# One more pair of feed-forward blocks per chunk pair in the seven-product down projection, and another order of the first chunk pair's blocks

## The chip, the cores and the metric

The kernel runs on one core of a Trainium2 chip. The metric is the device time of one execution in microseconds (us); the time before is the median of three runs. A core has these engines, which run side by side and wait for each other by semaphores: TensorE (PE, matmuls), VectorE (DVE), ScalarE (ACT), GpSimd (POOL) and SyncE (SP, which here issues nearly all DMA transfers). PSUM is the memory in which matmuls leave their results; DVE and ACT read it, POOL does not in this kernel.

## The reference

One pre-norm transformer layer in float32 on 2048 tokens of width 640: attention of 32 heads, then a SwiGLU feed-forward part of width 1728.

```
x = A_x
h = x + _A_ref(_layernorm(x, axis=-1), A_wqkv, A_wo)
h2 = h + _B_ref(_layernorm(h, axis=-1), B_w_gate, B_w_up, B_w_down)
...
def _B_ref(x, w_gate, w_up, w_down):
    g = _silu(x @ w_gate)
    u = x @ w_up
    return (g * u) @ w_down
```

## The kernel before

Projections, attention and the output projection take the first three quarters of the span; the change concerns the feed-forward part behind them, and the splitting of the down weights, which POOL does in tasks spread over attention (`prepare_weights`).

**Numbers.** To keep float32 accuracy every matmul operand is split into a high and a low part (`split`: ACT writes the high part, POOL or DVE the low one), and a product is the sum of high x high, high x low and low x high: three matmuls.

**Tiling.** The 2048 tokens form four chunks of 512 (0 to 3), taken as two *chunk pairs*, pair 0 (chunks 0, 1) and pair 1 (chunks 2, 3). The width 1728 forms 14 blocks f: 0 to 12 are whole (128 columns), 13 is half (64). `ELEMENTS` lists (pair, f): for each pair first block 13, then 0 to 12, so 28 elements, numbered 0 to 27. An element computes the gate and up products of one block for both chunks of its pair (`blocks`; `plain` for block 13), 54 matmuls of 512 columns over eight steps (30 over six steps for block 13), and leaves y = silu(gate) x up for the first chunk ahead of its step 5 and for the second ahead of its step 7 (block 13: steps 2 and 5). Steps are called by element and number here: step 4.5 is element 4, step 5, counted from 0. The order of the whole stage is written out by hand: the tile framework runs under a manual schedule, so each engine executes its instructions in the order of the program.

**Down products.** A block's y is multiplied by its down weights for four *tile pairs* (tp 0 to 3, two tiles of 128 tokens each; tp 0 and 1 are the pair's first chunk). Work for one tile pair is a `Group`, and groups wait in the list `waiting`. A group of one block (`plain` in `Group`, for blocks for which `own` holds) has four products of three matmuls of 320 columns (two for block 13), and DVE adds each to h, the residual, in SBUF. A group of two blocks (`seven`) forms the 2x2 by 2x2 block product of two tiles, two blocks and two halves of the output with seven products in place of eight; three products are added to h, four to sums kept aside (`sums`, tiles named own). Before, pair 0 takes blocks 0, 1, 12 and 13 alone and 2 to 11 as pairs; pair 1 takes 10 to 13 alone and 0 to 9 as pairs.

A group of two needs its operands prepared (`prepare`): ACT splits and POOL adds and splits into tiles named yp, from a pool that is opened (`opened`) only when the list `late` is empty. `late` holds the work that turns chunks 2 and 3 into the layout of the products (normalise, transpose on PE, `sums` and `keep`, and stores to DRAM, among them those of the tile named kept), one entry per step; it empties in step 4.3. The memory of that work is then reused by yp. Blocks whose y is needed before that are split at once (`EARLY`).

After the last group of two, `put_together` appends eight POOL additions per tile pair to the list `chores`, which combine the sums aside with h. Then h is complete but for the blocks that are still to come; the last block's `plain` stores it to the output. Chunks 2 and 3 have no place of their own in the feed-forward part: their h lies in DRAM (h_d), and `bring_back` reloads it into the place of chunk 0 or 1 once that is stored.

**What sets the order.** After the up matmuls of each step, `step()` refills the weight rings on the SP queue (`unit_ring` of eight up-weight units, `down_ring` of ten down-weight pieces), calls `bring_back`, takes as many down products from `waiting` as `RATES` says for that element (14 by default, spread over its steps; a second number gives the first step), prepares, pops two chores, and pops one entry of `late`. What is left at the end is taken in the last loop over `waiting`. SP works in order too: a store that waits for POOL holds the loads behind it. Down products use four PSUM banks (ps_b), up products four others (ps_a); PE waits when DVE has not emptied one.

Of the kernel before, what the change touches and what calls it, by code (L numbers as in the profile page):

```python
# [11 lines left out]
F32R = mybir.dt.float32r  # L12
# [5 lines left out]
P = 128  # L18
# [9 lines left out]
TPC = CH // P  # L28
NF = (F + P - 1) // P
# [6 lines left out]
HALF = D // 2  # L36
# [8 lines left out]
def tile_block(ctx: ExitStack, tc: tile.TileContext, x, wqkv, wo, wg, wu, wd, out):  # L45
    nc = tc.nc
    x = x[0]
    out = out[0]
    ctx.enter_context(tc.manual_schedule())

    dram = ctx.enter_context(tc.tile_pool(name="dram", bufs=1, space=bass.MemoryType.DRAM))
# [9 lines left out]
    t_d = [dram.tile([P, 8 * CH], F32R, name=f"t_d{i}") for i in range(2)]  # L61
    w_d = [dram.tile([P, 8, 4 * P], F32R, name=f"w_d{f}") for f in range(NF)]
    d_d = {
        f: dram.tile([P, 2, 2 * HALF], F32R, name=f"d_d{f}") for f in (0, 1, *range(NF - 4, NF))
    }
    j_d = [dram.tile([P, 7, 2 * HALF], F32R, name=f"j_d{j}") for j in range((NF - 2) // 2)]
    h_d = dram.tile([2, P, TPC, D], F32, name="h_d")
# [903 lines left out]
    h_c = {c: pe1.tile([P, TPC, D], F32, name=f"h{c}") for c in range(2)}  # L971
# [302 lines left out]
        def free(self, n=1):  # L1274
            self.freed += n

    ELEMENTS = [(pair, f) for pair in range(2) for f in (NF - 1, *range(NF - 1))]

    def weight_rings():
        def unit(f, i):  # L1280
# [103 lines left out]
    for u in range(NU):  # L1384
        g, c = divmod(u, NC)
        if g == NG - 1 and c >= 2:
            _, first, ln, flips, _ = ahead
# [143 lines left out]

    def own(pair, f):

        return f >= NF - 4 if pair else f < 2 or f >= NF - 2

    SLOTS = ("A11", "A12", "A22", "S1", "S2", "S3", "S4")
    sums, chores, stored = {}, [], []
    waiting, pools = [], []

    class Group:  # L1540
# [48 lines left out]
        def seven(self, n):  # L1589
            name, _, place = SEVEN[n]  # L1590
            if self.tp == 0:
                self.d.append(down_ring.take())
            d, k = self.d[n], SLOTS.index(name)
            y_hi, y_lo = self.parts[:, 0, k], self.parts[:, 1, k]
            ps = self.multiply([(y_hi, d[:, 0]), (y_hi, d[:, 1]), (y_lo, d[:, 0])])
            if self.tp == 3:
                down_ring.free()
            if isinstance(place, tuple):
                self.add(ps, *place)
            else:  # L1600
                own_sum = sums[self.tp][place]
                if self.fs[0] == (2, 0)[self.pair]:
                    nc.vector.tensor_copy(own_sum, ps)
                else:
                    nc.vector.tensor_tensor(out=own_sum, in0=ps, in1=own_sum, op=ALU.add)
            if n == 6 and own(self.pair, self.fs[1] + 1):
                self.put_together()

        def put_together(self):

            h = h_c[self.c]
            at = [h[:, self.t + i, k * HALF : (k + 1) * HALF] for i in range(2) for k in range(2)]
            one, six, seven, five = sums[self.tp]
            for out, x in (
                (at[0], one), (six, one), (at[1], six), (at[1], five), (seven, six),
                (at[2], seven), (five, seven), (at[3], five),
            ):
                chores.append((
                    self.pair, self.tp,
                    lambda o=out, x=x: nc.gpsimd.tensor_tensor(out=o, in0=o, in1=x, op=ALU.add),  # L1620
                ))

        def plain(self, n):
            i, half = divmod(n, 2)
            if len(self.d) < 2:
                self.d.append(down_ring.take())
            d = self.d[half]
            cols = slice((self.t + i) * P, (self.t + i + 1) * P)
            if self.fs[0] == NF - 1:
                y = self.parts[:, cols]  # L1630
                pairs = [(y, d[:, 0]), (y, d[:, 1])]
            else:
                if isinstance(self.parts, tuple):
                    y_hi, y_lo = (y[:, cols] for y in self.parts)
                else:
                    y_hi, y_lo = self.parts[:, 0, i], self.parts[:, 1, i]
                pairs = [(y_hi, d[:, 0]), (y_hi, d[:, 1]), (y_lo, d[:, 0])]
            ps = self.multiply(pairs)
            if self.tp == 3 and i == 1:
                down_ring.free()  # L1640
            self.add(ps, i, half)
            if self.fs[0] == NF - 2 and half == 1:
                while any(c[:2] == (self.pair, self.tp) for c in chores):
                    chores.pop(0)[2]()
                tt = self.c * TPC + self.t + i
                nc.sync.dma_start(out[tt * P : (tt + 1) * P, :], h_c[self.c][:, self.t + i, :])
                if self.pair == 0:
                    stored.append((self.c, self.t + i))

    def prepare_some():  # L1650
        for n, g in enumerate(waiting[:3]):
# [3 lines left out]
    def next_down():  # L1655
        if not waiting:
            return
        g = waiting[0]
        prepare_some()
        f, i = g.steps.pop(0)  # L1660
        f(i)
        if not g.steps:
            waiting.pop(0)
# [127 lines left out]
    plan = []  # L1791
    for pair, f in ELEMENTS:
        if own(pair, f):
# [116 lines left out]
    def spread_over(n, steps, first=0):  # L1910
# [1 line left out]
        return [0] * first + [n * (i + 1) // m - n * i // m for i in range(m)]  # L1912

    RATES = {
# [3 lines left out]
    }  # L1918
    again = []

# [5 lines left out]
        again[:] = stored  # L1926
        stored.clear()

    EARLY = ((0, 0), (0, 1))

    def y_place():
        return pd2.tile([P, CH], F32, name="y", tag="y", bufs=7)
# [1 line left out]
    for e, (pair, f) in enumerate(ELEMENTS):  # L1934
# [5 lines left out]
        def step():  # L1940
# [12 lines left out]
            for _ in range(each[n]):  # L1953
                next_down()
            prepare_some()
            for _ in range(2):
                if chores:
                    chores.pop(0)[2]()
            if soon:
# [39 lines left out]
        before = ys  # L1999
    while waiting:  # L2000
        next_down()


_INS = ["A_x", "A_wqkv", "A_wo", "B_w_gate", "B_w_up", "B_w_down"]
# [26 lines left out]
```

## Time and profile before

| | |
|---|---|
| median of 3 runs | 2010.2 us (2009.26 to 2012.54) |
| the profiled execution's own time | 2009.57 us |
| its span in the trace | 2007.8 us |
| DVE, ACT and POOL busy | 80%, 71%, 40% of the span |
| feed-forward stage, elements 1 to 27 | from about 1492 us to the end |

The span is the time from the first to the last instruction in the trace. A row of the timeline reads: start in us, length in us, engine, line, operation, what is written and read, how many such instructions follow each other, and in brackets the engine's idle time before the row and what ended it. A row of a stretch reads: its bounds and length, then for PE, PEld (weight loads), DVE, ACT and POOL the busy us and the number of instructions, then the clock granted to PE, the busy share of the DMA engines and GB/s. A row of a group reads: busy us, mean ns of one, and idle time before.

### The profile page before, as it was taken

What the parts mean: (1) busy time and instruction counts of PE and PEld (TensorE: products, weight loads), DVE (VectorE), ACT (ScalarE), POOL (GpSimd) and SP (SyncE); (2) the same over time, 40 slices, a digit from 0 to 9 for tenths busy, and PEclk for the clock granted to TensorE, in tenths of its full rate; (3) what the DMA queues carried; (4) which work ended last, traced back from release to release, by engine and by line L of the source; (5) the groups of instructions that cost most, each with busy time, mean ns of one, the idle gap of its engine ahead of it and who ended that gap; (6) DMA issues with size and microseconds to landing.
All of it is one profiled execution on the core that took longest, in us unless ns stands there. A gap on an engine that the chain in (4) does not pass through costs nothing.

```text
span 2007.8 us, 40038 instructions
## 1 busy us (share of the span) xinstructions
PE 1998.6 (100%) x14346; PEld 1246.9 (62%) x14346; DVE 1603.0 (80%) x2806; ACT 1434.3 (71%) x2811; POOL 799.2 (40%) x1206
## 2 busy tenths in 40 slices
PE   9999999999999999999999999999999999999999
PEld 8999995333333333333334333345598888888888
DVE  5778778898898888989888989886387766676677
ACT  4678778999999999999999999986633222212221
POOL 7574423344343443453400020011156444854555
PEclk9999999999999999999999999999999999999999
DMA  8887563442634534435412031221158654974642
GB/s 250 259 265 258 180 218 82 128 147 92 188 107 140 154 128 145 157 121 178 154 50 77 27 94 53 79 63 62 50 189 300 227 181 161 358 266 158 205 150 94
DMA packets 201541, 310.98 MB, mean 155 GB/s; under 512 B 55960, under 2 KB 89816, under 8 KB 200320
## 3 DMA queue, kind: packets, MB, share of 16 engines
q1 hardware_dynamic: 194752, 284.83, 43.6%
q0 software_dynamic: 6496, 23.60, 3.9%
q8 instruction: 114, 1.87, 0.4%
q14 instruction: 83, 0.68, 0.1%
q10 hardware_dynamic: 96, 0.00, 0.0%
HBM read 208.73 MB, written 99.32 MB: 153 GB/s over the span
## 4 chain that ended last, share of the span: by engine, by line
PE 97%; DMA 1%; DVE 1%; POOL 1%; ACT 0%; issue 0%; SPq 0%; ACTq 0%; POOLq 0%; DVEq 0%
PE acc L1319 25%; PE ps_a L1487 17%; PE ps_one L1309 16%; PE ps_max L274 13%; PE ps_one L647 10%; PE ps_b L1582 9%; PE ps_max L239 3%; PE ps_max L1037 2%; PE ps_b L1037 1%; DMA q_d<-e 0%; PE ps_two L700 0%; PE ps_max L1072 0%; DMA o_t<-o_d 0%; PE ps_a L1853 0%; DVE st L139 0%
## 5 line engine op out<-in xcount | busy, mean ns | idle before, releaser
L1315 ACT ACTIVATE probs<-ps_one 128x512 f32<-128x512 f32 x2048 | 1056.0, 614 | 58.7 <-PE ps_one L1309 33.9
L280 DVE TENSOR_REDUCE mx<-ps_max 128x1 f32<-128x512 f32 x1472 | 924.8, 683 | 104.5 <-PE ps_one L1309 79.0
L1309 PE MATMUL ps_one<-q_stk,k_stk 62*128 62x512 f32 x2048 | 579.4, 448 | 0.3 <-ACT probs L1315 0.3
L1319 PE MATMUL acc<-probs,v_stk 128*32 128x512 f32 x4096 | 546.2, 604 | 0.0
L1309 PEld LDWEIGHTS ps_one<-q_stk,k_stk 62*128 62x128 f32 x2048 | 247.5, 184 | 441.8 <-ACT probs L1315 419.9
L274 PE MATMUL ps_max<-k_stk,q_stk 60*128 60x512 f32 x1472 | 373.9, 425 | 0.1
L274 PEld LDWEIGHTS ps_max<-k_stk,q_stk 60*128 60x128 f32 x1472 | 272.9, 186 | 25.4 <-DVE mx L280 0.6
L1704 DVE TENSOR_TENSOR tmp<-ps_a,tmp 128x512 f32<-128x512 f32 x208 | 141.2, 689 | 121.0 <-PE ps_a L1487 92.9
L261 DVE TENSOR_REDUCE mx<-ps_max 128x2 f32<-128x512 f32 x288 | 180.7, 684 | 60.8 <-PE ps_max L239 56.1
L1319 PEld LDWEIGHTS acc<-probs,v_stk 128*32 128x32 f32 x4096 | 80.9, 108 | 178.9 <-issue 166.7
L251 ACT ACTIVATE ps_max<-ps_max 128x512 f32<-128x512 f32 x288 | 151.9, 584 | 39.6 <-PE ps_max L239 38.4
L1582 PE MATMUL ps_b<-halves,yp 128*128 128x320 f32 x1032 | 178.7, 308 | 0.2 <-DVE h L1587 0.2
L1582 PEld LDWEIGHTS ps_b<-halves,yp 128*128 128x128 f32 x1032 | 165.1, 188 | 16.0 <-DVE h L1587 0.5
L1487 PE MATMUL ps_a<-t,units 128*128 128x512 f32 x624 | 162.5, 396 | 0.0
L1354 POOL TENSOR_TENSOR o<-o,rb 128x512 f32<-128x512 f32 x31 | 39.9, 1286 | 268.9 <-DMA q_stk<-m_d 145.3
L90 POOL TENSOR_TENSOR yp<-y,yp 128x256 fp32r<-128x256 f32 x96 | 60.3, 628 | 187.0 <-ACT yp L89 187.0
L1487 PE MATMUL ps_a<-z,units 128*128 128x512 f32 x516 | 133.9, 394 | 0.0
L1487 PEld LDWEIGHTS ps_a<-t,units 128*128 128x128 f32 x624 | 112.6, 188 | 18.5
L295 POOL CAST neg<-neg 128x16 fp32r<-128x16 f32 x30 | 5.9, 196 | 282.7 <-DVE neg L287 282.7
L1587 DVE TENSOR_TENSOR h<-ps_b,h 128x320 f32<-128x320 f32 x248 | 109.7, 480 | 5.8 <-PE ps_b L1582 4.4
L647 PE MATMUL ps_one<-z_hi,w_lo 64*128 64x512 f32 x380 | 111.9, 392 | 0.0
L647 PE MATMUL ps_one<-z_hi,w_hi 64*128 64x512 f32 x380 | 111.7, 393 | 0.0
(220 smaller groups left out, 2752.7 us busy)
## 6 DMA issues: line engine op xcount, KB each, us to landing
units<-w_d SPq DMA_DIRECT2D x186, 256.0 KB
w_d<-stage SPq DMA_DIRECT2D x106, 256.0 KB
halves<-j_d SPq DMA_DIRECT2D x70, 320.0 KB
j_d<-stage SPq DMA_DIRECT2D x42, 320.0 KB
raw<-k_d SPq DMA_DIRECT2D x64, 160.0 KB
k_stk<-k_d SPq DMA_DIRECT2D x64, 160.0 KB
q_stk<-q_d SPq DMA_DIRECT2D x64, 160.0 KB
raw<-q_d SPq DMA_DIRECT2D x54, 160.0 KB
```

The source lines that it names most:

```text
L251: nc.scalar.activation(ps, ps, AF.Relu)
L261: nc.vector.tensor_reduce(mx[:, b, :, t, kc], ps.rearrange("p (j n) -> p j n", j=2), axis=AX.X, op=ALU.max,)
L274: nc.tensor.matmul(ps, queries[u][rows, pair, t * P : (t + 1) * P], keys[u // NC][rows, pair, kc * CH : (kc + 1) * CH], start=True, stop=True,
L280: nc.vector.tensor_reduce(mxs[u][:, b, pair, t, kc : kc + 1], ps, axis=AX.X, op=ALU.max)
L647: nc.tensor.matmul(ps, a[rows], b[rows], start=(i == n == 0), stop=(i == 1 and n == last), skip_group_check=True,)
L1309: nc.tensor.matmul(ps, keys[u // NC][rows, p, kt * P : (kt + 1) * P], queries[u][rows, p, :], start=True, stop=True,)
L1315: nc.scalar.activation(probs[p][:, b, :], ps, AF.Exp, scale=scale)
L1319: nc.tensor.matmul(acc[32 * j : 32 * j + 32, :], values[u // NC][:, kt, j * VW : j * VW + 32], probs[j // 2][:, j % 2, :], start=(kt == 0) ...
L1487: nc.tensor.matmul(ps.rearrange("p (t n) -> p t n", t=TPC), w[k][:, i], z[k][:, :, j], start=(first and m == 0), stop=(last and m == len(n ...
L1582: nc.tensor.matmul(ps, a, b, start=(n == 0), stop=(n == len(pairs) - 1))
L1587: nc.vector.tensor_tensor(out=h, in0=ps, in1=h, op=ALU.add)
L1704: add = lambda out, ps, x: nc.vector.tensor_tensor(out=out, in0=ps, in1=x, op=ALU.add)
```

## The change

All pairs of whole blocks but the last whole block go through the seven products, in both chunk pairs: blocks 0 to 11 as six pairs, 12 and 13 alone. Pair 0 now begins with blocks 13 and 12, then 0 to 11; only block 12 is split at once (`EARLY`). Pair 0 therefore ends with a put-together, and the stores of its h become chores behind it (`finish`); in pair 1 block 12 stays last and stores as before. The rates of elements 1 to 5, 15, 16 and 25 to 27 are others, four chores are popped per step in elements 14, 15, 16 and 27 in place of two, and the last loop pops one chore per product. The separate down weights of blocks 0, 1, 10 and 11 (d_d) are no longer split and stored; the pairs' weights (j_d) were stored for all six pairs before, too.

```diff
     d_d = {
-        f: dram.tile([P, 2, 2 * HALF], F32R, name=f"d_d{f}") for f in (0, 1, *range(NF - 4, NF))
+        f: dram.tile([P, 2, 2 * HALF], F32R, name=f"d_d{f}") for f in range(NF - 2, NF)
     }
...
-    ELEMENTS = [(pair, f) for pair in range(2) for f in (NF - 1, *range(NF - 1))]
+    ELEMENTS = [(0, f) for f in (NF - 1, NF - 2, *range(NF - 2))]
+    ELEMENTS += [(1, f) for f in (NF - 1, *range(NF - 1))]
...
     def own(pair, f):
 
-        return f >= NF - 4 if pair else f < 2 or f >= NF - 2
+        return f >= NF - 2
...
-                if self.fs[0] == (2, 0)[self.pair]:
+                if self.fs[0] == 0:
                     nc.vector.tensor_copy(own_sum, ps)
...
+            for i in range(2) if self.pair == 0 else ():
+                chores.append((self.pair, self.tp, lambda i=i: self.finish(i)))
...
-            if self.fs[0] == NF - 2 and half == 1:
+            if (self.pair, self.fs[0]) == (1, NF - 2) and half == 1:
                 while any(c[:2] == (self.pair, self.tp) for c in chores):
                     chores.pop(0)[2]()
-                tt = self.c * TPC + self.t + i
-                nc.sync.dma_start(out[tt * P : (tt + 1) * P, :], h_c[self.c][:, self.t + i, :])
-                if self.pair == 0:
-                    stored.append((self.c, self.t + i))
+                self.finish(i)
+
+        def finish(self, i):
+            tt = self.c * TPC + self.t + i
+            nc.sync.dma_start(out[tt * P : (tt + 1) * P, :], h_c[self.c][:, self.t + i, :])
+            if self.pair == 0:
+                stored.append((self.c, self.t + i))
...
     RATES = {
-        1: (10, 2), 2: (12, 0), 3: (13, 0), 4: (13, 0), 5: (14, 2), 6: (13, 0),
-        14: (12, 0), 15: (16, 0), 16: (16, 0),
-        25: (18, 0), 26: (22, 0), 27: (26, 0),
+        1: (8, 2), 2: (10, 0), 3: (11, 0), 4: (13, 4), 5: (15, 0),
+        14: (12, 0), 15: (18, 0), 16: (15, 0),
+        25: (14, 0), 26: (18, 0), 27: (30, 0),
     }
...
-    EARLY = ((0, 0), (0, 1))
+    EARLY = ((0, NF - 2),)
...
-            for _ in range(2):
+            for _ in range(4 if e in (14, 15, 16, 27) else 2):
                 if chores:
                     chores.pop(0)[2]()
...
     while waiting:
         next_down()
+        if chores:
+            chores.pop(0)[2]()
```

Three places of the instructions' order follow; rows give line, operation, what is written and read, the size, and a count. In the changed kernel the lines lie one to eight further down (1582 becomes 1583, 1620 becomes 1621).

PE around its first product from a prepared operand (yp). Before, from step 4.6 to step 5.2:

```order
L1487 MATMUL ps_a<-z_1_5625,units 128x512 x6
L1487 MATMUL ps_a<-z_1_5625,lasts 128x512 x3
L1582 MATMUL ps_b<-halves,y 128x320 x6
L1487 MATMUL ps_a<-z_1_5625,lasts 128x512 x3
L1582 MATMUL ps_b<-halves,y 128x320 x6
L1487 MATMUL ps_a<-z_0_5624,units 128x512 x6
L1487 MATMUL ps_a<-t_21742,units 128x512 x6
L1487 MATMUL ps_a<-z_0_5624,units 128x512 x6
L1487 MATMUL ps_a<-z_0_5624,lasts 128x512 x3
L1582 MATMUL ps_b<-halves,yp 128x320 x6
```

Now, from step 4.0 to step 4.5:

```order
L1488 MATMUL ps_a<-z_0_5620,units 128x512 x6
L1488 MATMUL ps_a<-t_21706,units 128x512 x6
L1488 MATMUL ps_a<-z_0_5620,units 128x512 x6
L1488 MATMUL ps_a<-z_0_5620,lasts 128x512 x3
L1488 MATMUL ps_a<-t_21705,units 128x512 x6
L1488 MATMUL ps_a<-t_21706,units 128x512 x6
L1583 MATMUL ps_b<-halves,y 128x320 x9
L1488 MATMUL ps_a<-t_21705,units 128x512 x6
L1488 MATMUL ps_a<-z_0_5620,lasts 128x512 x3
L1583 MATMUL ps_b<-halves,yp 128x320 x9
```

The first product from yp stands in element 4 in place of element 5, two steps behind the last entry of `late`, and the first four steps of element 4 hold up products alone.

SP where pair 1's h takes the place of pair 0's (out is the output, h_d the h of pair 1 in DRAM). Before, from element 15 on:

```order
L1924 DMA h_5622<-h_d 128x640
L1646 DMA out<-h_5623 128x640
L1265 DMA lasts<-w_d_79 128x512
L1924 DMA h_5623<-h_d 128x640
L1646 DMA out<-h_5623 128x640
L1265 DMA units<-w_d_78 128x512
L1924 DMA h_5623<-h_d 128x640
L1646 DMA out<-h_5623 128x640
L1265 DMA units<-w_d_78 128x512
L1265 DMA halves<-j_d_96 128x640
L1924 DMA h_5623<-h_d 128x640
```

Now, the last two tile pairs of pair 0:

```order
L1652 DMA out<-h_5619 128x640 x2
L1265 DMA lasts<-w_d_79 128x512
L1265 DMA halves<-j_d_92 128x640 x2
L1265 DMA units<-w_d_78 128x512
L1265 DMA halves<-j_d_92 128x640 x3
L1930 DMA h_5619<-h_d 128x640 x2
L1265 DMA units<-w_d_78 128x512
L1265 DMA halves<-j_d_93 128x640
L1652 DMA out<-h_5619 128x640 x2
L1265 DMA units<-w_d_78 128x512 x2
L1930 DMA h_5619<-h_d 128x640 x2
```

A store used to follow DVE's addition of block 12, tile by tile; now two stores follow POOL's eight additions of a tile pair, and the reloads come behind them.

POOL at the end of the program (h<-h,own and own<-own are the additions of `put_together`, yp<-y of 128x256 the split for a plain group). Before:

```order
L90 TENSOR_TENSOR yp<-y,yp 128x256
L1620 TENSOR_TENSOR h_5623<-h_5623,own 128x320
L1620 TENSOR_TENSOR own<-own 128x320
L1620 TENSOR_TENSOR h_5623<-h_5623,own 128x320 x2
L90 TENSOR_TENSOR yp<-y,yp 128x256
L1620 TENSOR_TENSOR own<-own 128x320
L1620 TENSOR_TENSOR h_5623<-h_5623,own 128x320
L90 TENSOR_TENSOR yp<-y,yp 128x256
L1620 TENSOR_TENSOR own<-own 128x320
L1620 TENSOR_TENSOR h_5623<-h_5623,own 128x320
L90 TENSOR_TENSOR yp<-y,yp 128x256 x4
```

Now:

```order
L1621 TENSOR_TENSOR own<-own 128x320
L1621 TENSOR_TENSOR h_5619<-h_5619,own 128x320
L1621 TENSOR_TENSOR own<-own 128x320
L1621 TENSOR_TENSOR h_5619<-h_5619,own 128x320
L90 TENSOR_TENSOR yp<-y,yp 128x256 x2
L1621 TENSOR_TENSOR h_5619<-h_5619,own 128x320
L1621 TENSOR_TENSOR own<-own 128x320
L1621 TENSOR_TENSOR h_5619<-h_5619,own 128x320 x2
L1621 TENSOR_TENSOR own<-own 128x320
L1621 TENSOR_TENSOR h_5619<-h_5619,own 128x320
L1621 TENSOR_TENSOR own<-own 128x320
L1621 TENSOR_TENSOR h_5619<-h_5619,own 128x320
```

The additions used to lie among the splits of the plain blocks 10 to 12, with four splits behind them. Now each tile pair's eight follow one another; between the four eights lie one preparation (of tile pair 3) and two times two splits, ahead of them the preparation of tile pair 2, and the last eight additions are the last that POOL does.

## The prediction

> **What bounds the kernel now.** First the page's engine line, then the table of stretches for the feed-forward stage from element 1 on.
>
> ```profile
> span 2007.8 us, 40038 instructions
> PE 1998.6 (100%) x14346; PEld 1246.9 (62%) x14346; DVE 1603.0 (80%) x2806; ACT 1434.3 (71%) x2811; POOL 799.2 (40%) x1206
> ...
> 1492.00:1995.00 503.00, 503.00 (x2612) 438.77 (x2612) 356.83 (x685) 118.22 (x254) 274.76 (x394) 1.00 0.63 213
> ```
>
> PE is busy in all 503.00 us of that stretch. A modelled busy time alone would not prove density, so I read starts in PE's timeline:
>
> ```profile
> 1569.15 0.86 PE L1487 MATMUL ps_a<-z,lasts 128*128 128x512 f32 x3
> 1569.84 1.04 PE L1582 MATMUL ps_b<-halves,yp 128*128 128x320 f32 x6
> 1570.72 1.56 PE L1487 MATMUL ps_a<-t,units 128*128 128x512 f32 x6
> 1572.12 1.03 PE L1582 MATMUL ps_b<-halves,yp 128*128 128x320 f32 x6
> ```
>
> Six matmuls of 320 columns advance PE by 1570.72 - 1569.84 = 0.88 us, 0.1465 each; six of 512 by 1.40, 0.233 each. Steps of the stage last the sum of these, so PE is the bound and nothing is waited for: a matmul removed is a matmul won, and every wait that is added is paid in full.
>
> **The change, part by part.** *Matmuls.* Two plain blocks cost a tile pair 2x4x3 = 24 matmuls, a seven-product pair 21. One pair of blocks more for each of 2 chunk pairs and 4 tile pairs: 8x3 = 24 matmuls fewer, 24 x 0.1465 = **-3.5 us**.
>
> *Weights.* Eight stores of d_d and their splits on POOL go, all during attention. Two equal stretches there, with and without such work:
>
> ```profile
> 900.00:934.00 34.00, 34.00 (x244) 13.49 (x240) 30.41 (x51) 33.30 (x67) 18.72 (x28) 1.00 0.56 187
> 1034.00:1068.00 34.00, 34.00 (x240) 13.14 (x232) 30.21 (x51) 33.08 (x66) 1.29 (x2) 1.00 0.29 86
> ```
>
> PE and ACT are full in both whether POOL has 18.72 or 1.29 us of work; the removal is worth 0. Between elements 5 and 13, and 17 and 25, POOL gets eight preparations more in all (40 us against the 228 that it is free in the stretch above) and the queue six weight loads; both stay behind PE, which is no nearer to them there than before: 0.
>
> *The first seven-product group (element 4).* It needs prepared operands (yp), whose memory is opened only after the late tokens' last store, in step 4.3. Before, PE asked for them in step 5.2; now in step 4.5. In between PE issued 33 matmuls of 512 and 48 of 320 columns: 33 x 0.233 + 48 x 0.1465 = 14.7 us, so PE asks at 1569.84 - 14.7 = 1555.1. When can they be there?
>
> ```profile
> 1541.09 0.71 PE L1853 MATMUL ps_a<-ident,z 128*128 128x128 f32 x5
> ```
> ```profile
> 1554.44 0.52 SPq L1812 DMA_DIRECT2D t_d<-halves  x1
> 1555.78 0.72 SPq L1812 DMA_DIRECT2D t_d<-kept  x1
> ...
> SPq L1265 <- DMA t_d<-kept: 0.4, 1, 0.4
> ```
> ```profile
> 1562.00 0.62 ACT L89 ACTIVATE yp<-y 128x256 fp32r<-128x256 f32 x2 [7.03 <-DMA units<-w_d]
> 1565.05 0.63 ACT L89 ACTIVATE yp<-tmp 128x512 fp32r<-128x512 f32 x1 [2.44 <-POOL tmp L1575]
> ```
> ```profile
> 1564.98 0.46 POOL L90 TENSOR_TENSOR yp<-y,yp 128x128 fp32r<-128x128 f32 x1
> 1565.76 1.30 POOL L90 TENSOR_TENSOR yp<-tmp,yp 128x512 fp32r<-128x512 f32 x1 [0.32 <-ACT yp L89]
> 1567.01 1.19 POOL L90 TENSOR_TENSOR yp<-y,yp 128x256 fp32r<-128x256 f32 x1
> ...
> 1570.73 1.29 POOL L90 TENSOR_TENSOR yp<-tmp,yp 128x512 fp32r<-128x512 f32 x1 [0.33 <-ACT yp L89]
> ```
>
> The kept store was issued at 1555.78. SP waited 0.4 us for it ahead of its next issue, and ACT began yp at 1562.00 after 7 us idle: yp lies where "kept" lay, so the store's 6.0 us gate it (the profile names another DMA; the one SP waited for fits better). From ACT's start to the last piece on POOL are 1567.06 - 1562.00 = 5.06 us. The chain to the store starts at the transposes of step 3.5 (1541.09); 15 down matmuls fewer stand ahead of these now, so it moves 2.2 us earlier and the pieces are complete at 1564.9. The second product's third matmul wants them at 1555.1 + 5 x 0.1465 = 1555.8. PE loses **9.0 us**. Bounds: 11 if the chain doesn't move; 6 if the store takes the 3.9 us of the "out" store below and ACT gets to the copy 0.7 us sooner. I take 9.0, since the 6.0 us is this very store. Ahead of PE's wait nothing helps: DVE and ACT have only work that PE feeds, and the next group's preparation is queued behind the first on POOL.
>
> [...]
>
> *The change of chunk pairs (elements 14 to 17).* Plain block 12 of pair 0 used to stand between the last put-together and pair 1, giving POOL time. Now pair 1's block 13 follows at once, and the rows of h that it adds to are first stored and reloaded.
>
> ```profile
> 1732.55 1.55 PE L1487 MATMUL ps_a<-z,units 128*128 128x512 f32 x6
> ```
> ```profile
> 1739.45 0.63 ACT L89 ACTIVATE y<-tmp 64x512 fp32r<-64x512 f32 x1 [0.83 <-DVE tmp L1676]
> ```
> ```profile
> L1620 POOL TENSOR_TENSOR h<-h,own 128x320 f32<-128x320 f32 x40 | 37.1, 930 | 2.6 <-DVE h L1587 0.2
> L1620 POOL TENSOR_TENSOR own<-own 128x320 f32<-128x320 f32 x24 | 21.5, 896 | 0.1
> ...
> 1756.41 0.88 POOL L1620 TENSOR_TENSOR own<-own 128x320 f32<-128x320 f32 x1
> 1757.37 1.71 POOL L1620 TENSOR_TENSOR h<-h,own 128x320 f32<-128x320 f32 x2
> 1759.04 0.87 POOL L1620 TENSOR_TENSOR own<-own 128x320 f32<-128x320 f32 x1
> 1759.87 0.73 POOL L90 TENSOR_TENSOR yp<-y,yp 128x256 fp32r<-128x256 f32 x1
> 1760.56 2.27 POOL L1620 TENSOR_TENSOR h<-h,own 128x320 f32<-128x320 f32 x2
> ```
> ```profile
> 1762.79 0.34 SPq L1646 DMA_DIRECT2D out<-h  x1
> ...
> 1766.73 0.32 SPq L1924 DMA_DIRECT2D h<-h_d  x1
> ```
>
> Prices: one put-together addition 0.9 us (64 take 58.6 busy; four run from 1756.41 to 1759.87), a preparation 5.0 (1567.01 to 1572.02), a plain split 0.7. In this stretch all is told without the delay of element 4, which shifts it as a whole. Step 14.0 starts at 1732.55, less 12 matmuls (1.8): 1730.8. ACT's half of block 13's first split ended at 1739.45 + 0.63, 7.5 us after that step began, and the same 15 and 12 matmuls stand before it now: POOL takes over at 1738.3. From there its program holds two such splits (1.4 each, as for 128x512 above), two preparations and 32 additions: 2.8 + 10.0 + 28.8 = 41.6, ending at 1779.9. Two out stores (0.4 between them) with 3.9 us to landing (1762.79 to 1766.73, where the reload waits for it), then a reload of the same size: h is back at about 1788.5. PE has 138 matmuls of 512 and 117 of 320 columns to step 16.7's products, 49.3 us, and ends the first that needs this h at 1780.4. DVE stops at its addition, with all later evictions queued behind; PE has four ps_b banks and goes on for three more products and 12 matmuls (0.9 + 2.8) to 1784.1, then waits for 1788.5: **4.5 us**. Bounds 0.5 (a reload in no time) to 8 (out and reload at the 6.0 us above). I take the 3.9 twice. Behind the store that waits on SP stand loads of up weights; they run a whole element ahead (54 x 0.233 + 42 x 0.1465 = 18.7 us), more than the 8 or so that SP is held.
>
> *The end.* Before, the put-together of pair 1 followed blocks 8 and 9, three plain blocks ahead of the end. Now it follows 10 and 11.
>
> ```profile
> 1964.67 1.56 PE L1487 MATMUL ps_a<-t,units 128*128 128x512 f32 x6
> ```
> ```profile
> 1967.75 0.95 DVE L1708 TENSOR_TENSOR y<-tmp 128x512 f32<-128x512 f32 x1
> 1997.29 7.07 DVE L1587 TENSOR_TENSOR h<-ps_b,h 128x320 f32<-128x320 f32 x17
> ```
>
> Step 26.5 starts at 1964.67, less 27 matmuls that are not yet issued there (4.0): 1960.7. The y of its first chunk follows 1968.7 - 1964.67 = 4.0 later, at 1964.7. Only then can POOL begin: four preparations 20.1, 32 additions 28.8, four plain splits 2.8, together 51.7, in a program without gaps, to 2016.4. By the matmuls alone DVE's last addition would end at 2004.36 - 3.5 = 2000.8; now it waits for POOL's. One addition (0.6) and the last store (2007.8 - 2004.36 = 3.4) end the span at 2020.4 where it was 2007.8: **+12.6**, the 3.5 us of saved matmuls included. Bounds: 8 if additions take their 0.84 best and the first preparations are hidden, 15 if more of them take the 1.2 or so that 1760.56 shows.
>
> *Sum.* 9.0 + 4.5 + 12.6 = 26.1 on the profiled execution's 2009.57 us (span 2007.8 and 1.8 around it): 2035.7. The median of the runs is 0.6 above that execution: **2036 us**.
>
> **The rivals.** (1) *Not slower*: POOL and the stores keep up, and only the matmuls count: 2010.2 - 3.5 = 2006.7. For it speaks that POOL is idle 60% of the span; against it that the average is not the end: its 51.7 us would have to fit into 2000.8 - 1964.7 = 36.1, so it decides at instructions of 0.70 of their rows. 4%. (2) *Only the end costs*: the kept store lands before step 4.5, h is reloaded in time: 2010.2 + 12.6 = 2023. It needs the store 9 us earlier; its chain hangs on PE's transposes. 14%. (3) *PE restarts slowly after each wait.* The warming matmuls at the kernel's start (L809) show it:
>
> ```profile
> 3.00:5.00 2.00, 2.00 (x12) 2.00 (x11) 1.00 1.09 383
> 7.00:10.00 3.00, 2.97 (x27) 2.77 (x25) 1.00 1.07 361
> ```
>
> 12 matmuls of 128 columns in 2 us, later 27 in 3: about 1.9 times slower at first, though the granted clock reads 1.00 in both. If a wait of 9 us brings that back for some 3 us, it costs 1.5, and the wait of 4.5 us perhaps as much: 2039. No wait of PE of that length stands in this trace. 25%. [...]
> (4) That the change doesn't do what it says is excluded by the order of instructions: 24 matmuls are gone.
>
> **How the numbers follow.** Forecast 2036 with 52%, rivals 1 to 3 with 4, 14 and 25%, 5% for waits that I have not seen (a longer time). The range 2020 to 2044 takes in the forecast with its bounds (2010.2 + 6 + 0.5 + 8 = 2025 below, + 11 + 8 + 15 = 2044 above) and rivals 2 and 3. A measurement of this kernel tells 0.2% from no change, 4 us: slower 0.94, same 0.04, faster 0.02 (rival 1, at -0.17%, lies just inside the border).
>
> **What would show it.** Element 4 right: an idle time of PE of 6 to 11 us ahead of its first product from yp, released by ACT, then POOL. The change of pairs right: DVE's h addition waiting for h<-h_d, and PE idle a few us in elements 16 or 17. The end right: POOL without gaps in the last 50 us, its additions to h the last but DVE's, PE done over 8 us before the end. Wrong: a PE that is full to the end, or the chain of waits naming weights.

## The result and the profile after

| | before | after |
|---|---|---|
| median | 2010.2 us (2009.3 to 2012.5) | 2044.5 us (2044.1 to 2047.5) |
| span of the profiled execution | 2007.8 us | 2045.7 us |
| mean granted TensorE clock in it | 1.000 | 0.994 |

The changed kernel is slower, by a ratio of 1.0171 (95% interval 1.0159 to 1.0183), 34.4 us. The forecast was 26 us more; the direction and each of the three waits came, but 8.5 us were missing from the sum, and the time lies half a microsecond outside the range.

The engine line of the changed kernel's page, and the row of the same stretch that stood first in the prediction (PE's busy us are the first figure behind the length; the clock is the third from the right):

```profile
span 2045.7 us, 40026 instructions
PE 2007.8 (98%) x14322; PEld 1249.2 (61%) x14322; DVE 1600.5 (78%) x2798; ACT 1438.6 (70%) x2821; POOL 810.7 (40%) x1232
...
1492.00:1995.00 503.00, 488.56 (x2491) 422.73 (x2490) 340.26 (x649) 117.75 (x252) 254.92 (x383) 0.99 0.64 216
```

PE was busy in all 503.00 us of that stretch; now it lacks 14.4 of them. What it waited for from 1492 on, in us in total, times, and the longest one (before, this list was one row of 0.2 us):

```profile
PE ps_b L1583 <- POOL yp L90: 10.7, 7, 3.1
PE ps_b L1583 <- ACT yp L89: 4.7, 1, 4.7
PE ps_b L1583 <- DVE h L1588: 3.3, 1, 3.3
PE ps_b L1583 <- DMA halves<-j_d: 2.9, 2, 2.0
PE ps_b L1583 <- ACT tmp L1723: 0.5, 1, 0.5
PE ps_a L1488 <- ACT tmp L1723: 0.5, 1, 0.5
```

Three rows answer to the forecast: ACT and POOL at yp (element 4 and the end), DVE at h (the change of pairs). The fourth, down weights, was not in it, and the prediction had named it among its signs of being wrong. The two short waits for ACT lie in steps 17.1 and 2.1. Waits are less than what is lost, though, since PE is also slow behind them. I therefore take, for each step, its length in PE's timeline less its matmuls at the dense pace (0.2326 us for 512 columns, 0.1462 for 320). Element 4:

```profile
1558.55 1.56 PE L1488 MATMUL ps_a<-t,units 128*128 128x512 f32 x6
1559.95 0.86 PE L1488 MATMUL ps_a<-z,lasts 128*128 128x512 f32 x3
1565.47 0.87 PE L1583 MATMUL ps_b<-halves,yp 128*128 128x320 f32 x2 [4.66 <-ACT yp L89]
1568.21 1.17 PE L1583 MATMUL ps_b<-halves,yp 128*128 128x320 f32 x3 [1.87 <-POOL yp L90]
1569.82 1.43 PE L1583 MATMUL ps_b<-halves,yp 128*128 128x320 f32 x4 [0.44 <-POOL yp L90]
1571.05 1.95 PE L1488 MATMUL ps_a<-z,units 128*128 128x512 f32 x6
```

Step 4.5 lasts 1571.05 - 1558.55 = 12.50 us for 9 matmuls of each kind, 3.41: 9.1 lost, and 0.4 more in step 4.6, whose first six matmuls took 1.95 in place of 1.56. The same reckoning over the whole stage finds all places above 0.35 us:

| place | forecast | lost in the trace |
|---|---|---|
| 24 matmuls fewer | -3.5 | -3.5 |
| step 2.1 | | 0.6 |
| element 4 | 9.0 | 9.5 (steps 4.5, 4.6) |
| element 14 (added loads of weights: 0) | 0 | 5.7 (1.5, 2.7, 1.4 in steps 14.3 to 14.5) |
| change of pairs | 4.5 | 5.9 (4.1, 1.0, 0.7 in steps 16.7, 17.0, 17.1) |
| end, without the matmuls | 16.1 | 14.9 |
| sum | 26.1 | 33.1 |

The end is 1.3 + 2.3 + 7.4 us in steps 26.7, 27.5 and the tail (0.7 of before taken off), and 4.0 because the span ends 8.0 us behind PE's last matmul where it was 4.0. From element 1 to the end the trace takes 2045.7 - 1496.3 = 549.4 us against 2007.8 - 1491.6 = 516.2 before: 33.2 more, so the table is complete. The other 4.7 us of the two spans' difference arose before the feed-forward part. By the first activation of attention (L1316), 319.63 against 316.28, 3.35 us are lost, in projections where this one execution waited for loads:

```profile
PE ps_max L239 <- DMA raw<-q_d: 2.0, 2, 1.4
```

About 1.6 more come right behind that, where its granted clock was 0.58 from 322 to 326, and 0.3 are won back by element 1. That is no part of the change: element 1 starts at 1490.6 to 1492.4 in eleven of the twelve kernels below (1493.9 in the other), and the three other executions of the changed kernel have spans of 2042.3 to 2042.9.

*The clock.* The same stretches show the granted clock (third figure from the right) around two of PE's waits:

```profile
1555.00:1560.00 5.00, 5.00 (x27) 4.26 (x26) 2.81 (x5) 1.67 (x3) 1.89 (x2) 1.00 0.70 249
1560.00:1565.00 5.00, 0.81 (x4) 0.32 (x2) 2.66 (x6) 0.24 (x1) 0.00 (x0) 1.00 0.96 298
1565.00:1571.00 6.00, 3.22 (x9) 2.45 (x10) 0.98 (x2) 1.51 (x5) 5.27 (x10) 0.51 1.03 379
1572.00:1577.00 5.00, 5.00 (x30) 4.56 (x29) 3.04 (x6) 1.77 (x4) 3.41 (x6) 1.00 0.29 88
...
1804.00:1807.00 3.00, 2.98 (x9) 2.61 (x10) 2.90 (x6) 1.14 (x3) 0.93 (x2) 0.50 0.94 364
```

So rival 3 came too, beside the forecast and not in its place: behind these waits PE starts again at half clock (0.51 and 0.50 in the rows from 1565 and 1804). In windows of 1 us each such dip amounts to 3.4 us at half (the sum of what is missing is 1.71 a dip), two of them in a row in element 4.

### The profile page after: what moved, and what is told of

It is laid out like the page before. It is cut to its first block, busy times and chain, and to the rows that moved or that the text cites. A ratio compares the mean times of both kernels' runs of the same rounds, so it can differ in the third digit from the quotient of the medians.

```text
span 2045.7 us, 40026 instructions
## 1 busy us (share of the span) xinstructions
PE 2007.8 (98%) x14322; PEld 1249.2 (61%) x14322; DVE 1600.5 (78%) x2798; ACT 1438.6 (70%) x2821; POOL 810.7 (40%) x1232
## 4 chain that ended last, share of the span: by engine, by line
PE 91%; DMA 3%; POOL 3%; DVE 1%; SPq 1%; ACT 1%; issue 1%; POOLq 0%; DVEq 0%; ACTq 0%
PE acc L1320 25%; PE ps_one L1310 15%; PE ps_a L1488 15%; PE ps_max L274 13%; PE ps_one L647 9%; PE ps_b L1583 7%; PE ps_max L239 3%; PE ps_max L1037 2%; PE ps_b L1037 2%; DMA raw<-k_d 1%; POOL h L1621 1%; POOL yp L90 1%; SPq L176 1%; POOL own L1621 0%; DMA halves<-j_d 0%
## 5 line engine op out<-in xcount | busy, mean ns | idle before, releaser
L1316 ACT ACTIVATE probs<-ps_one 128x512 f32<-128x512 f32 x2048 | 1055.9, 613 | 60.7 <-PE ps_one L1310 35.7
L274 PEld LDWEIGHTS ps_max<-k_stk,q_stk 60*128 60x128 f32 x1472 | 272.9, 186 | 26.5 <-DVE mx L280 0.7
L1583 PE MATMUL ps_b<-halves,yp 128*128 128x320 f32 x1056 | 188.9, 313 | 19.0 <-POOL yp L90 10.7
L1583 PEld LDWEIGHTS ps_b<-halves,yp 128*128 128x128 f32 x1056 | 171.8, 191 | 38.9 <-POOL yp L90 12.8
L89 ACT ACTIVATE yp<-tmp 128x512 fp32r<-128x512 f32 x48 | 30.3, 632 | 129.7 <-POOL tmp L1576 129.7
L1588 DVE TENSOR_TENSOR h<-ps_b,h 128x320 f32<-128x320 f32 x208 | 95.6, 482 | 25.9 <-PE ps_b L1583 14.3
```

Of the source, the lines that this page charges most:

```text
L274: nc.tensor.matmul(ps, queries[u][rows, pair, t * P : (t + 1) * P], keys[u // NC][rows, pair, kc * CH : (kc + 1) * CH], start=True, stop=True,
L1316: nc.scalar.activation(probs[p][:, b, :], ps, AF.Exp, scale=scale)
L1583: nc.tensor.matmul(ps, a, b, start=(n == 0), stop=(n == len(pairs) - 1))
L1588: nc.vector.tensor_tensor(out=h, in0=ps, in1=h, op=ALU.add)
```

## Experiments

Each kernel is the changed one with the edit shown (excerpts), unless it says otherwise. Times are medians of four or five runs, beside runs of the kernel before on the same chip, whose medians lie between 2009.6 and 2011.0. Gains are told against the 2044.5 above, so differences of a microsecond or so between two kernels are not told apart.

**Which half of the change.** Pair 1 as before the change, then pair 0 as before it.

```diff
-        return f >= NF - 2
+        return f >= (NF - 4 if pair else NF - 2)
...
-        25: (14, 0), 26: (18, 0), 27: (30, 0),
+        25: (18, 0), 26: (22, 0), 27: (26, 0),
```

> Pair 1 as in the kernel before (blocks 10 and 11 alone, rates and additions of the end as before); pair 0 as changed. Theory A (the forecast's end is right at +12.6, and what the forecast missed lies in elements 4 to 17): the kernel before, 2010.2, less 12 matmuls (1.75), plus element 4 (9.5), elements 14 to 17 (5.7 and 5.8 in the changed trace) and about 1 ahead of the feed-forward part: about 2030.5. Theory B (the 8.5 us that the forecast missed are lost at the end): 2010.2 - 1.75 + 9.0 + 4.5 = 2022.

2031.7 us (2030.1 to 2032.2), ratio 1.0103 [1.0086, 1.0120]: theory A. The trace has the losses of element 4, element 14 and the change of pairs (9.9, 6.1 and 7.2 us by steps), and at the end no more than before (0.7).

```diff
-    ELEMENTS = [(0, f) for f in (NF - 1, NF - 2, *range(NF - 2))]
-    ELEMENTS += [(1, f) for f in (NF - 1, *range(NF - 1))]
+    ELEMENTS = [(pair, f) for pair in range(2) for f in (NF - 1, *range(NF - 1))]
...
-        return f >= NF - 2
+        return f >= NF - 2 if pair else f < 2 or f >= NF - 2
```

> Pair 0 as in the kernel before (blocks 0, 1, 12 and 13 alone, its order, rates and early splits); pair 1 as changed. Theory A: only the end costs, with 12 matmuls saved in place of 24: 2010.2 + 12.6 + 1.75 - 1 (POOL's stretch was 54.7 us in place of 55.7 to the end) = about 2023.5, and the granted clock is 1.00 but for the last 25 us. Theory B (the loss that the forecast missed lies at the end): 2032.

2023.6 us (2022.6 to 2025.6), ratio 1.0065 [1.0050, 1.0080]: theory A again. Only the end is lost (15.7 us by steps, all in element 27, of which 0.7 were lost before, too), and there the plain splits queue behind POOL's additions:

```profile
2009.57 3.57 PE L1582 MATMUL ps_b<-halves,yp 128*128 128x320 f32 x12 [5.11 <-POOL yp L90]
```

The two halves cost 21.7 and 13.6 us over 2010, together 35.3 where the whole change costs 34.4: they add to within a microsecond. For pair 1 the forecast has 12.6 + 1.75 = 14.4, so what it missed belongs to pair 0.

**Element 14.** The new wait, first on SP, then on PE, in the changed kernel:

```profile
1745.99 1.19 SPq L1265 DMA_DIRECT2D halves<-j_d  x2
1747.22 0.48 SPq L1911 DMA_DIRECT2D t<-t_d  x1
1747.80 1.89 SPq L1265 DMA_DIRECT2D halves<-j_d  x2
```
```profile
1754.30 1.50 PE L1583 MATMUL ps_b<-halves,yp 128*128 128x320 f32 x6 [0.90 <-DMA halves<-j_d]
1755.64 0.86 PE L1488 MATMUL ps_a<-z,lasts 128*128 128x512 f32 x3
1758.48 1.68 PE L1583 MATMUL ps_b<-halves,yp 128*128 128x320 f32 x6 [1.98 <-DMA halves<-j_d]
1759.95 2.77 PE L1488 MATMUL ps_a<-z,units 128*128 128x512 f32 x6
```

Four pieces for blocks 10 and 11 are issued just when the operands of the second chunk pair are loaded, a transfer of 1 MB between them, and PE wants them 7 to 9 us later. Before, no such piece was issued in this stretch; these two SP rows of the kernel before follow each other among the rows for halves, 26.5 us apart:

```profile
1718.36 0.74 SPq L1265 DMA_DIRECT2D halves<-d_d  x1
...
1744.91 0.42 SPq L1265 DMA_DIRECT2D halves<-d_d  x1
```

Since block 12 no longer stands behind them, blocks 10 and 11 are one element later in pair 0, and their weights fall among these loads.

```diff
-        ... 14: ("T2", "", "T1", "", "T3"), 15: ("T4",),
+        ... 14: ("", "", "", "", "T2", "T1"), 15: ("T3 T4",),
```

> The changed kernel, with the loads of the second chunk pair's first operand sums (t32 and t14, two of 1 MB in steps 14.0 and 14.2, one in 14.4) moved to steps 14.4, 14.5 and 15.0. If the down weights of blocks 10 and 11 came late in element 14 because they shared the queue and the DMA engines with these loads: PE's wait of 2.9 us for halves goes, and the half clock behind it: about 5.7 less, 2039. Rival 1 (the ring of ten pieces frees its slots too late, whatever else is loaded): 2044.5. Rival 2 (the operand sums now come late themselves): PE waits for t in element 15, 2041 or more.

2039.8 us (2038.9 to 2040.7), 4.7 less than the changed kernel, as forecast by the contention theory. In its trace all four pieces are issued in one go, ahead of the operands, and PE waits for no weights and no t:

```profile
1741.78 2.36 SPq L1265 DMA_DIRECT2D halves<-j_d  x4
...
1748.19 1.17 SPq L1911 DMA_DIRECT2D t<-t_d  x2
```

Element 14 loses 1.2 us by steps in place of 5.7. So of the 5.7 the waits for weights and the half clock behind them are about 4.5; the 1.2 stay with no wait in the list, and their cause is open. The same edit moves the loads out of the queue and out of the DMA engines at once; which of the two held the pieces up was not separated.

**Element 4.** Two ways to take its wait away. First, ask later:

```diff
-        1: (8, 2), 2: (10, 0), 3: (11, 0), 4: (13, 4), 5: (15, 0),
+        1: (8, 2), 2: (8, 0), 3: (8, 0), 4: (8, 0), 5: (16, 2), 6: (22, 0),
```

> The changed kernel, with rates 8, 8, 8, 8, 16 (from step 2) and 22 in elements 1 to 6, so that the first product from a prepared operand stands in step 5.2 as before the change; all else as changed. If element 4 loses its time to the store of kept and the preparation behind it: no wait of PE there and no stretch at half the granted clock around 1565 to 1572, about 9.5 less: 2035. Rival: y tiles are held longer, and DVE waits for one of the seven buffers in element 5 or 6: 2040 or more, with a new wait of DVE there.

2042.1 us (2041.8 to 2043.3): a miss, 2.4 won of 9.5: the rival's time, but not by the wait for y buffers that the rival names. The wait for yp in element 4 goes, but three others come. In step 5.3 DVE, and PE behind it, wait for ACT, whose eviction of a product is queued behind a split of the second preparation that POOL has not fed yet:

```profile
1568.43 1.49 DVE L1710 TENSOR_TENSOR tmp<-ps_a,tmp 128x512 f32<-128x512 f32 x2 [3.17 <-ACT tmp L1723]
```

In step 3.0 the transposes wait (1.4 us). And with 70 products taken by the end of element 6 where the changed kernel takes 71, the preparation of the third tile pair of blocks 10 and 11 comes one step later in POOL's program, behind a split that cannot start:

```profile
1754.06 1.29 POOL L90 TENSOR_TENSOR y<-tmp,y 64x512 fp32r<-64x512 f32 x1 [8.05 <-ACT y L89]
```

so that the change of pairs loses 9.9 us in place of 5.9. One product more or less moves an instruction past another that waits.

Second, let the place be free sooner: the three staging tiles of the late work rotate, and another start makes kept the last but two, so that the last two stores leave from the ring of down weights.

```diff
-        kept = [0]
+        kept = [2]
```

> The changed kernel, with another start of the rotation of the three staging tiles of the late work, so that the last use of the tile kept (whose place yp takes) is three stores earlier, and the last two stores leave from the ring of down weights. If the landing of the store of kept gates the first preparation: ACT starts on yp about 5.5 us sooner (near 1559 in place of 1564.8, relative to the same start), and part of that comes back as PE's wait for down weights, whose slots the last stores now hold: 2 to 6 us less than 2044.5, 2040. Rival: yp waits for other work of the late list (a last split on DVE or POOL), and the start of ACT's copy moves by less than 2 us: 2044.

2039.8 us (2039.0 to 2041.7), 4.7 less. In the changed kernel the store of kept and ACT's start on yp stand 5.8 us apart:

```profile
1559.01 0.72 SPq L1818 DMA_DIRECT2D t_d<-kept  x1
```
```profile
1564.76 0.61 ACT L89 ACTIVATE yp<-y 128x256 fp32r<-128x256 f32 x2 [7.45 <-issue]
```

With kept free earlier, ACT starts as soon as DVE has done the last split, ahead of the last store (issued at 1554.32, out of halves), 62.0 us behind the start of element 1 where it was 68.5:

```profile
1553.57 0.62 ACT L89 ACTIVATE yp<-y 128x256 fp32r<-128x256 f32 x2 [0.97 <-DVE halves L90]
```

Step 4.5 loses 4.9 us in place of 9.1, 1.7 of them for weights, whose slots the last stores now hold; 2.1 are lost in step 4.6, at half clock, where it was 0.4. Element 4 thus gains 2.4 us; the whole stage from element 1 on is 2.8 shorter in this trace, and the rest of the 4.7 is not located. The store's landing gated element 4, as the prediction read from a row that the profile had put down to another DMA.

**Who sets the end and the change of pairs.** Half of the additions on DVE:

```diff
+            engine = nc.vector if self.tp % 2 else nc.gpsimd
...
-                    lambda o=out, x=x: nc.gpsimd.tensor_tensor(out=o, in0=o, in1=x, op=ALU.add),
+                    lambda o=out, x=x: engine.tensor_tensor(out=o, in0=o, in1=x, op=ALU.add),
```

> The changed kernel, with the additions of put_together of the second and fourth tile pair on DVE in place of POOL (32 of 64). If POOL's additions are what the end and the change of chunk pairs wait for: POOL's stretch at the end falls from 50.4 us by 16 x 0.88 to about 36, PE's waits of 11.6 us there go, and the span ends about 14 earlier; h is reloaded in time for step 16.7, another 5.8: 2044.5 - 14 - 5.8 = 2025. Rival: the additions stand in DVE's order between evictions and wait for the other engines' parts there, so that DVE takes POOL's place as the bound: 2035 or more, with PE waiting for DVE.

2036.8 us (2034.8 to 2037.7): 7.7 won of the 20 expected, the rival's time. The wait of step 16.7 goes, but 1.4 us in step 15.7 are new and 1.6 in step 17.1 stay. At the end PE now waits for DVE too, up to 2.4 us. The groups of additions in the last 52 us of this kernel (busy us, mean ns):

```profile
L1622 POOL TENSOR_TENSOR h<-h,own 128x320 f32<-128x320 f32 x10 | 9.0, 905 | 0.6
...
L1622 DVE TENSOR_TENSOR h<-h,own 128x320 f32<-128x320 f32 x10 | 6.6, 656 | 0.2
...
L1622 POOL TENSOR_TENSOR own<-own 128x320 f32<-128x320 f32 x6 | 6.0, 997 | 0.0
...
L1622 DVE TENSOR_TENSOR own<-own 128x320 f32<-128x320 f32 x6 | 5.2, 863 | 0.0
```

An addition on DVE is no 0.48 us, as it is where POOL is idle (at 1786.57 in this trace), but 0.66 to 0.86 in the mean. The three edits of half_dve, kept_first and later_swaps were then put together:

> half_dve, kept_first and later_swaps together. If the costs are separate and add: 2044.5 - 19.8 - 4.5 - 4.7 = 2015.5, still slower than before (2010.2). If the waits of one are hidden behind another's, each removed one shows the next: 2020 or more.

2030.3 us (2028.5 to 2031.2), where the second theory puts it. But by the measured gains (7.7, 4.7, 4.7) it would have been 2027.4: they nearly add, and the size of the first was wrong.

**The half clock.** In later_swaps, matmuls whose result nobody reads fill the two long waits:

```diff
+            if (e, n) in FILL:
+                ps = bank()
+                for _ in range(FILL[e, n]):
+                    nc.tensor.matmul(ps[:, :P], ident, ident, start=True, stop=True)
             for _ in range(each[n]):
                 next_down()
...
+    FILL = {(4, 5): 40, (16, 7): 28}
```

> The kernel later_swaps (2039.8) with 40 matmuls of 128 columns on the identity, whose result nobody reads, ahead of the first product from yp in step 4.5, and 28 ahead of the products of step 16.7: PE does something in the two waits. If the half clock behind a wait costs what PE's rows show (3.4 us at half each, 1.6 us where PE is the bound, less where PE waits on anyway): the granted clock stays at 1.00 from 1500 to 1990 and the time falls by 1.5 to 3, to 2037 to 2038.5. Rival (the granted clock's dip is a sign of the wait, not a cost): 2040, or more by what the added matmuls outlast the waits.

2038.2 us (2037.4 to 2039.7). Each of these matmuls is two in the trace; they fill the wait, and the clock is 1.00 from 1500 to 2009:

```profile
1555.29 9.09 PE L1963 MATMUL ps_a<-ident 128*128 128x128 f32 x80
1564.14 1.66 PE L1583 MATMUL ps_b<-halves,yp 128*128 128x320 f32 x9
```

The 28 outlasted their wait, so 15 in their place:

> As swaps_warm (2038.2), with 15 added matmuls in step 16.7 in place of 28 (the 28 took 6.4 us there, the wait that they fill 3.75). If the half clock behind the wait costs PE 1.5 us or so in steps 17.0 and 17.1 (1.41 and 0.57 above the dense pace in later_swaps): these two steps come down to less than 0.6 together, step 16.7 takes what the wait takes, no dip of the granted clock between 1500 and 1990, and the median is 2037, 3 below later_swaps. Rival (the dip costs nothing that PE would not wait anyway): 2039.5 to 2040.

2038.3 us (2036.9 to 2041.7), between the two expectations. Step 17.0 is at the dense pace now, where later_swaps lost 1.4, but PE then stands in step 17.1, and a dip follows that wait:

```profile
1803.09 0.68 PE L1583 MATMUL ps_b<-halves,yp 128*128 128x320 f32 x3 [1.80 <-ACT yp L89]
```

The filled waits take 1.5 us off the median of later_swaps, no more than the runs of one kernel scatter. That PE runs at half pace behind a wait is shown by rows (1805.25 below); how much of it the kernel would have lost anyway is left open.

**Is there a version that beats both?** From pair0_before, which saves 12 matmuls and loses only at the end: the additions of the first and third tile pair on DVE; the preparation of blocks 10 and 11 one group earlier, meant for the fourth tile pair; both.

```diff
+            engine = nc.gpsimd if self.tp % 2 or self.pair == 0 else nc.vector
...
-            if n < 2 or len(g.fs) == 1:
+            if n < 2 or len(g.fs) == 1 or (g.pair, g.fs[0]) == (1, NF - 4):
```

> The kernel pair0_before (2023.6: pair 0 as before the change, pair 1 as changed), with pair 1's additions of put_together of the first and third tile pair on DVE in place of POOL. If POOL's work in a row sets the end: 16 x 0.88 = 14 us fewer on POOL; the stretch in which only POOL works behind PE (5.1 and 1.5 us of PE's waits, 3 at half clock) goes, and PE's waits for the fourth tile pair's preparation (1.8 and 0.8) too, since the first pair's additions no longer stand ahead of it on POOL: 2012 to 2014. Rival (DVE is the bound there, as in half_dve): 2018 or more.

2017.3 us (2016.5 to 2017.9), 6.3 less than pair0_before, between the two expectations: PE waits for POOL no more, but 5.5 us for DVE:

```profile
2003.33 7.67 PE L1582 MATMUL ps_b<-halves,yp 128*128 128x320 f32 x39 [2.82 <-DVE h L1587]
```

> The kernel pair0_before (2023.6) with the fourth tile pair of blocks 10 and 11 of pair 1 prepared one group earlier, ahead of the first tile pair's additions on POOL; all additions stay on POOL. If the end is POOL's sum of work, the order within it is worth little: PE's waits of 1.8 and 0.8 us in step 27.5 go and come back at the end, 2023. Rival (the order counts: PE is fed earlier, its last products and DVE's additions lie ahead of POOL's last): 2019 or less.

2026.5 us (2024.7 to 2028.0), slower by 2.9, by neither expectation. PE loses 7.0 us in steps 27.0 and 27.1. The condition moves the second tile pair's preparation too: it now stands on ACT ahead of a silu (L1751) that came before it in pair0_before, and a split in it waits for POOL. So the silu waits, DVE behind it, and PE behind DVE:

```profile
1973.30 0.63 ACT L89 ACTIVATE yp<-tmp 128x512 fp32r<-128x512 f32 x1 [3.34 <-POOL tmp L1575]
1973.83 0.61 ACT L1751 ACTIVATE tmp<-tmp 128x512 f32<-128x512 f32 x1
...
1974.48 1.34 DVE L1711 TENSOR_TENSOR y<-tmp 128x512 f32<-128x512 f32 x1 [5.09 <-ACT tmp L1751]
...
1976.27 1.97 PE L1582 MATMUL ps_b<-halves,yp 128*128 128x320 f32 x6 [4.46 <-DVE h L1587]
```

Moving the fourth preparation alone was not tried.

> end_dve and end_prep together: the best that these runs point to. PE without waits in the last 50 us would give 2010.2 - 1.75 = 2008.5, 0.1% faster than before, which is less than can be told; with a wait or two left 2010 to 2013. Rival (DVE's order holds PE's banks up): 2016 or more.

2022.3 us (2020.8 to 2024.3), 5.0 more than end_dve and the rival's time: steps 27.0 and 27.1 lose 6.3 us as in end_prep, and PE waits for DVE. None beats the kernel before; the nearest, end_dve, is at 1.0036 [1.0022, 1.0050].

## What the prediction had right, and the step that failed

- *Bound by PE, a wait is paid in full*: right. The changed kernel's 33 us in the feed-forward part are the sum of PE's losses by steps and the longer tail behind it.
- *Matmuls, -3.5*: right. 24 fewer stand in the trace, at the same pace.
- *Element 4, 9.0*: right in mechanism (kept_first) and size, 9.5. The chain went as told: store, ACT's split, POOL's preparation, PE.
- *Change of pairs, 4.5*: right in mechanism, 5.9 in size. DVE waited 4.80 us for the reload, PE 3.3 (forecast: a wait of PE of 4.5):

```profile
1803.48 0.89 DVE L1588 TENSOR_TENSOR h<-ps_b,h 128x320 f32<-128x320 f32 x2 [4.80 <-DMA h<-h_d]
```
```profile
1799.84 0.86 PE L1488 MATMUL ps_a<-z,lasts 128*128 128x512 f32 x3
1804.02 1.44 PE L1583 MATMUL ps_b<-halves,y 128*128 128x320 f32 x4 [3.32 <-DVE h L1588]
1805.25 2.55 PE L1488 MATMUL ps_a<-z,units 128*128 128x512 f32 x6
```

  Behind it six matmuls of 512 columns took 2.55 us in place of 1.56. The forecast had the half clock as a rival and left it out of the sum.
- *The end*: right in mechanism and near in size. POOL started its first preparation with block 11's y and ran almost without a gap to its last addition, then DVE's and the store:

```profile
1991.57 0.74 POOL L90 TENSOR_TENSOR yp<-y,yp 128x256 fp32r<-128x256 f32 x1 [9.66 <-ACT yp L89]
...
2041.11 0.86 POOL L1621 TENSOR_TENSOR h<-h,own 128x320 f32<-128x320 f32 x1
```

  That is 50.4 us where 51.7 were forecast, and the end costs 14.9 us with the matmuls apart, where 16.1 were forecast; pair0_before has it alone.
- *The step that failed* is the term of weights, "eight preparations more in all ... and the queue six weight loads; both stay behind PE, which is no nearer to them there than before: 0". It counts the loads that are added in elements 5 to 13 and 17 to 25, and does not ask when the loads of the blocks that are *moved* take place. Blocks 10 and 11 move one element back, their last four pieces meet the loads of the operands, and element 14, for which the sum has no term, loses 5.7 us, 4.5 of which later_swaps gives back by steps. The clue stood in the trace before: SP's rows between 1718 and 1745 hold no load of halves.
- The half clock, which the forecast had as a rival and left out of the sum, is contained in these losses: 0.4 us in step 4.6, 1.4 in step 14.5, 1.0 in step 17.0, outside the end. The range's upper end, 2044, was made of the bounds of three waits alone, with no room for a fourth one.
- The sentence that behind SP's waiting store stand loads of up weights leaves out the down weights that stand there, too (the order of SP ahead of the prediction shows them). It cost nothing: in elements 15 to 17 PE waits for no weights.
- Of the 8.5 us missed, then: element 14 5.7, the change of pairs 1.4, step 2.1 0.6, element 4 0.5, the end -1.2, in all 7.0; 1.5 remain between the trace's sum and the medians. In step 2.1 PE waits 0.5 us for an eviction on ACT, which stands behind a split that waited 1.6 us for POOL. Step 2.1 and that rest were not tried.

## What to carry to other kernels

Where one engine is full, list for a moved block every transfer that moves with it, and lay it beside what else is on the queue at the new place; a count of the loads that are added says nothing about that. In these traces an instruction that waited held everything behind it on its engine, so an operation moved past a waiting one can cost more than the work that it saves: with one product fewer by the end of element 6 (later_seven) the change of pairs lost 9.9 us where it was 5.9, and a preparation one group earlier (end_prep) made the whole 2.9 us slower. A scheme that saves 3.5 us on the full engine has to bring its side work to a place where the side engines have room; here the last 50 us had too little: half of the additions moved from POOL to DVE gained 6.3 us there (end_dve), and PE then waited 5.5 us for DVE.

## What the runs showed of the hardware

- The kernel before has a granted clock of 1.00 throughout. In the changed kernel it is 0.50 behind four of the five waits of PE over 1.9 us, in pieces of 3.4 us: two in a row behind the wait of 4.66, one each behind those of 1.98, 3.32 and 2.68. The dip of element 14 (1759.6 to 1763.0, in rows of 0.1 us) followed waits of 0.9 and 2.0 us with work between them, and began 1.1 us after PE had started again. Behind the wait of 3.12 us at the end (2034.26) the clock stays 1.00, so the length of the last wait alone does not tell whether a dip follows. And at the start of attention, near 320 us, three of the thirteen changed kernels' traces have a dip and the others and the kernel before have none; PE's wait for ACT's probs there is 0.2 or 0.3 us with a dip (all three) and 0.3 us without one (the kernel before, pair0_before, pair1_before, later_seven); what brings it there was not shown.
- In half_dve, DVE's addition of h and own, which both lie in SBUF, lasts 0.48 us beside an idle POOL (1786.57 to 1788.02, 2024.98 to 2027.38). Over the last 52 us, in most of which POOL adds and splits, it lasts 0.66 (h) and 0.86 (own) in the mean, up to 1.55 (2008.90). POOL's own additions last 0.91 (h) and 1.00 (own) there, where both are 0.87 in pair0_before. In end_dve the means are 0.67 and 0.71 on DVE, 0.88 and 1.00 on POOL. So at the end of half_dve 16 additions on DVE took 11.8 us, where 16 x 0.48 would be 7.7, and the 16 left on POOL 15.0, where 16 x 0.87 would be 13.9. What slows the two beside each other was not shown.
